# Moving the key and value loads, one split and two score products in the first 35 passes of an attention-then-two-MLPs kernel

## The chip, the cores and the metric

The program runs on one core of one Trainium2 chip, in one launch. The metric is the device time of one execution in microseconds (us), from the runs of the kernel as a whole. Five engines work side by side, each through its own instructions in order: PE (TensorE, matmuls), DVE (VectorE), ACT (ScalarE), POOL (GpSimd) and SP (SyncE, which here issues all DMAs). Semaphores tie them together.

## The reference

For 8 batches, 8 heads, 576 tokens and head width 64, the keys and values are averaged over groups of 8 tokens (576 to 72), and each token attends to the 72 pooled ones. The result, 4608 tokens by 512, goes through two MLPs (512 to 2048 to 512) with a gate each.

```python
k_p = k.reshape(B, H, Sp, pool, D).mean(axis=3)
v_p = v.reshape(B, H, Sp, pool, D).mean(axis=3)
scores = scale * np.matmul(q, k_p.transpose(0, 1, 3, 2))
...
attn = attn / (np.sum(attn, axis=-1, keepdims=True) + 1e-09)
return np.matmul(attn, v_p).astype(np.float32)
...
h = x @ w_in
g = h * (1.0 / (1.0 + np.exp(-h)))     # second MLP: h * clip(h + 3, 0, 6) / 6
return (g @ w_out).astype(np.float32)
```

## The kernel before

The 4608 tokens are 36 tiles of 128 (tile t holds rows 128t to 128t+127, so tile 9 is the first of batch 2 and tile 13 the first with rows of batch 3). Four tiles make a group of 512 tokens, nine groups in all. The kernel has three stretches: attention together with the first layer of the first MLP (to about 493 us), that MLP's second layer (L805), and the second MLP (L721, L821). The change lies in the first stretch.

**Passes.** That stretch is a list of passes n. Pass n computes one block of 128 hidden features for one group: `h_mm`, 12 matmuls of 128x512 at L628 into one of four PSUM banks. Passes 0 to 6 take features 0 to 6 of group 0, passes 7 to 13 the same of group 1, passes 14 to 22 the rest of group 0, 23 to 31 the rest of group 1; then one group after the other. Passes 0 to 6 run in `opening`, the others in the loop below it. Each pass's product goes through a tanh on ACT (L641) and a product on DVE (L642), both written in the next pass, and a store to DRAM on SP (L646). Because there are four banks, pass n needs that DVE product of pass n-4.

**A weight block** is split into two parts once: scale on ACT (L126), three bit operations on DVE (L133, L136, L140), head on ACT (L147), tail on DVE (L152). From pass 24 on, pieces of other weights are prepared in the same way in `pair_slots` (ACT L185, DVE L191 to L198, ACT L214, DVE L218) with sums on POOL (L223).

**An attention tile t** takes these steps, each in a pass that the table `todo` fixes: scores on PE (L458, 8 matmuls into two banks `aps`), maxima on DVE (L502, L505), eight exponentials on ACT (L512), which free the two banks, normalization on DVE (L529 to L533), transposes in blocks of 32 on DVE (L566), which a DMA takes to DRAM (L571, called "out" here) and three DMAs bring back reordered (L577, "back"), the product with the pooled values on PE (L592, `weighted`), and a split of the result into two parts on ACT (L608) and DVE (L609). For group 2 (tiles 8 to 11) the passes of scores and `weighted` are the table

```python
s, w = ((12, 25), (16, 26), (18, 28), (20, 29))[i]
```

with the maxima and exponentials in s+1, the normalization and transposes in s+3, "out" in s+4 and "back" in s+5.

**Keys and values of batch b**, four pieces j each, are loaded in the passes of `kv_in`, k and v together, and pooled on POOL three passes later (`pool_k`: L381, L382, two of L385; `pool_v`: L402, L403, L404). All k pieces share one staging tile and all v pieces another, so a load waits on SP until POOL is through with the piece before; everything that stands behind it on SP waits too. In a pass, the loads stand ahead of the "out" and "back" jobs (`due`) and of the stores (`later`). On POOL, the poolings of a pass stand behind the L223 sums of that pass.

**Before pass 0** the tiles 0 to 3 are worked off; the values of batch 0 are pooled by matmuls with the identity (`summed_v`, L395) for j = 0 and 3, and by POOL for j = 1 and 2. `keep_warm` (L444) issues idle matmuls, `WARM[t+1]` of them ahead of tile t's transposes.

Of the kernel before, what the change touches and what calls it, by code (L numbers as in the profile page):

```python
# [19 lines left out]
POOL = 8  # L20
GT = 512
G2 = 576
WARM = (16, 0, 4, 6)
FILL = 288


# [1 line left out]
def kernel(  # L28
# [815 lines left out]
    for t in range(TPG, NTILE):  # L844
        g, i = divmod(t, TPG)
        if g == 1:
            if i > 1:
                todo.setdefault(i - 1, []).append(("scores", t))
            for n, what in ((i, "soft"), (i + 1, "norm"), (i + 1, "probs"), (max(i + 2, 3), "weighted"), (max(i + 3, 4), "split")):
                todo.setdefault(n, []).append((what, t))  # L850
            continue
        if g == 2:
            s, w = ((12, 25), (16, 26), (18, 28), (20, 29))[i]
        else:
            w = NF * (g - 1) + (4, 7, 10, 13)[i]
            s = w - 10
        start[t] = s
        jobs = [(s, "scores"), (s + 1, "soft"), (w, "weighted"), (w + 1, "split")]
        jobs += [(s + 3, "norm"), (s + 3, "turn")]
        for n, what in jobs:  # L860
            if n >= 0:
                todo.setdefault(n, []).append((what, t))
    kv_in = {}
    for b in range(2, B):
        for j in range(NPAIR):
            n = 6 + 2 * j if b == 2 else start[first_tile[b]] - 18 + 4 * j
            assert n not in kv_in
            kv_in[n] = (b, j)
    stages = {}
    for f in range(1, NF):  # L870
        n = f - 1 if f < FIRST else (6, 7, 8, 10, 11, 13, 15, 17, 19)[f - FIRST]
# [4 lines left out]
    with tc.manual_schedule():  # L876
# [32 lines left out]
        for i in range(2):  # L909
            nc.gpsimd.memset(prs[i][:, H * SP:], 0.0)  # L910
        pool_k(0, 3, nc.gpsimd)
        for j in range(1, NPAIR - 1):
            pool_v(0, j)
        banks = [
            [(ps_a, "a"), (ps_a, "a")], [(ps_h, "h"), (ps_h, "h")],
            [(ps_y, "y0"), (ps_y, "y1")], [(ps_y, "y2"), (ps_y, "y3")],
# [19 lines left out]
        def soft(t):  # L936
            new_pr(t, f"o{4 + t}")
            if t < 1:
                max_exps(t, 0, False)
            else:  # L940
                below_max(t, 0)
                exps(t, 0)
            max_exps(t, 1)

        def turn(t):
            if t < 3:
                norm(t, 1 if t else 2)
            probs_T(t, banks[t], f"o{t}", WARM[t + 1] if t < 3 else 0)

# [8 lines left out]
        nc.scalar.activation(*outer, AF.Copy)  # L958
        scores(3, banks[3])
        soft(2)  # L960
        turn(1)
        soft(3)
        split_scale(0)
# [45 lines left out]
        def opening(n, f, now):  # L1009

            def factor(part, run):
                for what, i in stages.get(n, ()):
                    if what == part:
                        run(i)

            ps = h_mm(0, f, n)
            for what, t in now:
                if what == "weighted":
                    i = t - TPG
                    pv[t] = weighted(t, (A, B2)[i // 2][i % 2:])  # L1020
            if n == 0:
                scores(TPG, A, parts=(1,))
                scores(TPG + 1, B2)
                load_q(TPG + 3)
                vps1.append(bank(C, 1))
                summed_v(vps1[0], 1, 0)
                factor("head", split_head)
                factor("head", split_tail)
            for what, t in now:
                if what == "norm":  # L1030
                    norm(t, 2)
            for what, t in now:
                if what == "soft":
                    all_max(t)
            if late_silu:
                silu(*late_silu.pop())
            late_silu.append((0, f, n, ps))
            if n == 1:
                nc.scalar.activation(vp[1][:, :2 * D], vps1.pop()[:SP, :2 * D], AF.Copy)
            for what, t in now:  # L1040
                if what == "split":
                    split_x(t, pv.pop(t))
            if n:
                factor("head", split_head)
                factor("head", split_tail)
            for what, t in now:
                if what == "soft":
                    new_pr(t)
                    all_exps(t)
            factor("bits", split_bits)  # L1050
            for what, t in now:
                if what == "probs":
                    probs_T(t, C)
            for what, t in now:
                if what == "scores":
                    scores(t, B2 if t % 2 else A)
                    load_q(t + 2)
            factor("scale", split_scale)

        for n, (g, f) in enumerate(order):  # L1060
# [3 lines left out]
            load_ahead(2)  # L1064
            if n >= BEGIN - 3:
                load_halves()
            if n in kv_in:
                load_k(*kv_in[n])
                load_v(*kv_in[n])
            for job in due.pop(n, ()):  # L1070
                job()
            while later:
# [1 line left out]
            now = todo.get(n, ())  # L1074
            if n < FIRST:
                opening(n, f, now)
                if n - 3 in kv_in:
                    pool_k(*kv_in[n - 3], nc.gpsimd)
                    pool_v(*kv_in[n - 3])
                continue  # L1080
            for what, t in now:
                if what == "soft":
# [39 lines left out]
                    split_tail(i)  # L1122
            if job:
                job[1](job[2])
            if n - 3 in kv_in:
                pool_k(*kv_in[n - 3], nc.gpsimd)
                pool_v(*kv_in[n - 3])
            if g == NG - 2 and f in (8, 10):
                next_wide(1)
            if g == NG - 1:  # L1130
# [311 lines left out]
```

## Time and profile before

| what | us |
|---|---|
| median of 3 runs (lowest, highest) | 1508.34 (1507.77, 1509.56) |
| the profiled execution, its own time | 1504.98 |
| its span, first to last instruction | 1503.2 |
| PE busy in the span | 1483.7 (99%) |
| DVE, ACT, POOL busy | 1235.9, 804.2, 325.3 |

The profile is of one execution, whose time is 3.36 us under the median of the runs. The span leaves out what lies around the first and last instruction (1.8 us). Matmuls are pipelined, so that a busy PE need not be one at its peak; its idle time, on the other hand, is time in which it waited. Times in the rows are counted from the start of the span.

### The profile page before, as it was taken

What the parts mean: (1) busy time and instruction counts of PE and PEld (TensorE: products, weight loads), DVE (VectorE), ACT (ScalarE), POOL (GpSimd) and SP (SyncE); (2) the same over time, 40 slices, a digit from 0 to 9 for tenths busy, and PEclk for the clock granted to TensorE, in tenths of its full rate; (3) what the DMA queues carried; (4) which work ended last, traced back from release to release, by engine and by line L of the source; (5) the groups of instructions that cost most, each with busy time, mean ns of one, the idle gap of its engine ahead of it and who ended that gap; (6) DMA issues with size and microseconds to landing.
All of it is one profiled execution on the core that took longest, in us unless ns stands there. A gap on an engine that the chain in (4) does not pass through costs nothing.

```text
span 1503.2 us, 30700 instructions
## 1 busy us (share of the span) xinstructions
PE 1483.7 (99%) x11562; PEld 1415.5 (94%) x11562; DVE 1235.9 (82%) x1883; ACT 804.2 (53%) x1779; POOL 325.3 (22%) x378
## 2 busy tenths in 40 slices
PE   8899999999999999999999999999999999999998
PEld 7678888888888999999999999999999999999998
DVE  7987789788776898888988698888876877777776
ACT  5755555556644544444443677777776444444443
POOL 6362443443011000000000343444440000000000
PEclk9999999999999999999999999999999999999999
DMA  9568889989789955555559866655689954444440
GB/s 308 194 187 266 265 275 295 292 288 315 253 305 373 358 190 183 180 180 179 186 169 355 294 217 207 203 195 199 207 260 320 375 158 142 140 142 142 138 138 29
DMA packets 225461, 342.17 MB, mean 228 GB/s; under 512 B 16800, under 2 KB 157984, under 8 KB 225312
## 3 DMA queue, kind: packets, MB, share of 16 engines
q1 hardware_dynamic: 225312, 340.20, 68.1%
q8 instruction: 91, 1.49, 0.4%
q14 instruction: 58, 0.48, 0.1%
HBM read 194.90 MB, written 145.23 MB: 226 GB/s over the span
## 4 chain that ended last, share of the span: by engine, by line
PE 93%; DMA 3%; DVE 3%; issue 1%; ACT 0%; SPq 0%; DVEq 0%; ACTq 0%
PE pl L805 22%; PE pl L821 22%; PE hps L628 22%; PE py L721 12%; PE pa L721 6%; PE ph L721 3%; PE aps L458 2%; PE aps L592 2%; DVE rw L136 1%; DMA wraw<-in_moe_w_in_dram 1%; DMA qT<-in_q_dram 1%; DMA ro<-in_v_dram 1%; DMA stage<-in_k_dram 1%; DMA stage<-in_v_dram 0%; DVE rs L642 0%
## 5 line engine op out<-in xcount | busy, mean ns | idle before, releaser
L628 PE MATMUL hps<-rx,whl 128*128 128x512 f32 x1728 | 388.5, 383 | 3.1 <-DVE rx L609 2.2
L628 PEld LDWEIGHTS hps<-rx,whl 128*128 128x128 f32 x1728 | 324.2, 190 | 51.4 <-issue 2.6
L805 PEld LDWEIGHTS pl<-rx,wst 128*128 128x128 f32 x3024 | 337.9, 192 | 0.1
L805 PE MATMUL pl<-rx,wst 128*128 128x256 f32 x3024 | 337.9, 275 | 0.0
L821 PE MATMUL pl<-wst,rx 128*128 128x256 f32 x3024 | 337.8, 275 | 0.0
L821 PEld LDWEIGHTS pl<-wst,rx 128*128 128x128 f32 x3024 | 337.8, 192 | 0.0
L223 POOL TENSOR_TENSOR rw<-rw 128x256 f32<-128x256 f32 x96 | 75.7, 796 | 580.1 <-DVE rw L218 550.1
L721 PE MATMUL py<-rx,wst 128*128 128x288 f32 x1152 | 151.8, 286 | 0.2 <-DVE rx L695 0.2
L642 DVE SCALAR_TENSOR_TENSOR rs<-rs,hps 128x512 f32<-128x512 f32 x144 | 98.0, 681 | 61.6 <-ACT rs L641 61.2
L721 PEld LDWEIGHTS py<-rx,wst 128*128 128x128 f32 x1152 | 145.4, 189 | 0.4 <-DVE rx L695 0.4
L791 ACT ACTIVATE rx<-ro 128x1024 fp32r<-128x1024 f32 x86 | 90.6, 1062 | 87.7 <-PE pl L805 35.6
L641 ACT ACTIVATE rs<-hps 128x512 f32<-128x512 f32 x144 | 86.5, 606 | 67.9 <-PE hps L628 67.6
L1158 DVE TENSOR_TENSOR rs<-rs,pl 128x512 f32<-128x512 f32 x90 | 61.6, 685 | 69.6 <-PE pl L821 47.2
L792 DVE TENSOR_TENSOR rx<-ro,rx 128x1024 fp32r<-128x1024 f32 x86 | 103.5, 1224 | 14.6 <-ACT rx L791 14.4
L512 ACT ACTIVATE pr<-aps,mxa 128x72 f32<-128x72 f32 x256 | 78.2, 331 | 45.9 <-DVE mxa L505 45.9
L1161 ACT ACTIVATE rs<-pl 128x512 f32<-128x512 f32 x36 | 21.6, 601 | 145.4 <-PE pl L821 76.1
L791 ACT ACTIVATE rx<-ra 128x1024 fp32r<-128x1024 f32 x70 | 73.7, 1064 | 47.1 <-PE pl L805 18.3
L792 DVE TENSOR_TENSOR rx<-ra,rx 128x1024 fp32r<-128x1024 f32 x70 | 83.3, 1219 | 9.8 <-ACT rx L791 9.8
L791 ACT ACTIVATE rx<-rb 128x1024 fp32r<-128x1024 f32 x63 | 66.3, 1062 | 44.5 <-PE pl L821 20.3
L214 ACT ACTIVATE rw<-rw 128x256 fp32r<-128x256 f32 x152 | 61.8, 417 | 45.0 <-POOL rw L223 24.0
L792 DVE TENSOR_TENSOR rx<-rb,rx 128x1024 fp32r<-128x1024 f32 x63 | 75.9, 1231 | 5.9 <-ACT rx L791 5.8
L218 DVE TENSOR_TENSOR rw<-rw 128x256 fp32r<-128x256 f32 x152 | 71.9, 482 | 8.5 <-ACT rw L214 8.5
(135 smaller groups left out, 2115.6 us busy)
## 6 DMA issues: line engine op xcount, KB each, us to landing
ws<-rw SPq DMA_DIRECT2D x152, 256.0 KB
wst<-ws SPq DMA_DIRECT2D x76, 512.0 KB
g<-rs SPq DMA_DIRECT2D x144, 256.0 KB
g<-rs SPq DMA_DIRECT2D x128, 288.0 KB
ro<-g SPq DMA_DIRECT2D x49, 512.0 KB
ra<-g SPq DMA_DIRECT2D x38, 512.0 KB
rb<-g SPq DMA_DIRECT2D x37, 512.0 KB
rw<-in_moe_w_out_dram SPq DMA_DIRECT2D x64, 256.0 KB
```

What stands on the lines that cost most here:

```text
L214: nc.scalar.activation(t[:, 0], mag, AF.Copy)
L218: nc.vector.tensor_tensor(out=t[:, 1], in0=mag, in1=t[:, 0].bitcast(F32), op=ALU.subtract)
L223: nc.gpsimd.tensor_tensor(out=out, in0=a, in1=b, op=op)
L512: nc.scalar.activation(p_t[t][:, a, i], s_t[t][a][:, i], AF.Exp, scale=ESCALE, bias=mx[:, h], accum_out=den_of(t)[:, h],)
L628: nc.tensor.matmul(ps, w[:, c, :], shuffled(x[:, c, :]), start=(c == 0 and n == 0), stop=(c == NKC - 1 and n == 2),)
L641: nc.scalar.activation(in_two(t), dealt(ps), AF.Tanh)
L642: nc.vector.scalar_tensor_tensor(out=in_two(t), in0=in_two(t), scalar=1.0, in1=dealt(ps), op0=ALU.add, op1=ALU.mult)
L721: nc.tensor.matmul(ps[j], w[:, j, a, c, :], shuffled(x[:, b, c, :]), start=(first and n == 0 and c == 0), stop=(n == 2 and c == 1), skip_g ...
L791: nc.scalar.activation(t[:, dd, 0], src, AF.Copy)
L792: nc.vector.tensor_tensor(out=t[:, dd, 1], in0=src, in1=t[:, dd, 0].bitcast(F32), op=ALU.subtract)
L805: nc.tensor.matmul(ps[:, c * HW:(c + 1) * HW], w[:, b, c * P:(c + 1) * P], shuffled(t[:, dd, a, i]), start=(dd == 0 and c == 0 and i == 0 ...
L821: nc.tensor.matmul(ps[:, c * HW:(c + 1) * HW], t[:, dd, a, i, c * P:(c + 1) * P], shuffled(w[:, b]), start=(dd == 0 and c == 0 and i == 0 ...
```

## The change

Five things change. (1) `kv_in` becomes two tables. For batch 2 the k pieces stay at passes 6, 8, 10, 12 and the v pieces move from these to 15, 17, 19, 21. For batch 3 both were at 11, 15, 19, 23; k is now at 13, 17, 21, 25 and v at 23, 25, 27, 29. Each is pooled three passes after its load. Later batches keep their passes. (2) Tile 7 is split (L608, L609) in pass 5, ahead of the exponentials and the bit operations of that pass, not in pass 6. (3) Scores of tile 10 move from pass 18 to 19 and of tile 11 from 20 to 22, and all that hangs on them moves along: maxima and exponentials, normalization, "out", "back", and the load of q two tiles on. Their `weighted` stays in passes 28 and 29. (4) Piece j = 2 of the values of batch 0 is pooled by eight matmuls and one copy on ACT (now L964), not by POOL. (5) The four idle matmuls ahead of tile 1's transposes go.

```diff
-WARM = (16, 0, 4, 6)
+WARM = (16, 0, 0, 6)
...
-            for n, what in ((i, "soft"), (i + 1, "norm"), (i + 1, "probs"), (max(i + 2, 3), "weighted"), (max(i + 3, 4), "split")):
+            for n, what in ((i, "soft"), (i + 1, "norm"), (i + 1, "probs"), (max(i + 2, 3), "weighted"), (max(i + 3, 4) - (i == 3), "last" if i == 3 else "split")):
...
-            s, w = ((12, 25), (16, 26), (18, 28), (20, 29))[i]
+            s, w = ((12, 25), (16, 26), (19, 28), (22, 29))[i]
...
-    kv_in = {}
+    k_in, v_in = {}, {}
     for b in range(2, B):
         for j in range(NPAIR):
-            n = 6 + 2 * j if b == 2 else start[first_tile[b]] - 18 + 4 * j
-            assert n not in kv_in
-            kv_in[n] = (b, j)
+            n = start[first_tile[b]] - 18 + 4 * j
+            for kv, at in ((k_in, {2: 6 + 2 * j, 3: 13 + 4 * j}), (v_in, {2: 15 + 2 * j, 3: 23 + 2 * j})):
+                at = at.get(b, n)
+                assert at > max(kv, default=0)
+                kv[at] = (b, j)
...
-        for j in range(1, NPAIR - 1):
-            pool_v(0, j)
+        pool_v(0, 1)
...
         soft(2)
+        v2 = bank(A, 1)
+        summed_v(v2, 0, 2)
+        nc.scalar.activation(vp[0][:, 4 * D:6 * D], v2[:SP, 4 * D:6 * D], AF.Copy)
         turn(1)
...
             for what, t in now:
+                if what == "last":
+                    split_x(t, pv.pop(t))
+            for what, t in now:
                 if what == "soft":
                     new_pr(t)
                     all_exps(t)
...
-            if n in kv_in:
-                load_k(*kv_in[n])
-                load_v(*kv_in[n])
+            if n in k_in:
+                load_k(*k_in[n])
+            if n in v_in:
+                load_v(*v_in[n])
...
-            if n - 3 in kv_in:
-                pool_k(*kv_in[n - 3], nc.gpsimd)
-                pool_v(*kv_in[n - 3])
+            if n - 3 in k_in:
+                pool_k(*k_in[n - 3], nc.gpsimd)
+            if n - 3 in v_in:
+                pool_v(*v_in[n - 3])
```

SP, passes 23 to 25 before: the last load of batch 3's keys and values (`stage_1433`, `stage_1435`), then "back" of tile 10 (`bl0`), "out" and "back" of tile 11 (`bl1`).

```order
L368 DMA stage_1433<-in_k_dram 128x576
L376 DMA stage_1435<-in_v_dram 72x1024
L577 DMA ro_187<-bl0_89 32x4x256 x2
L577 DMA ro_187<-bl0_89 8x4x256
L646 DMA g0_0_175<-rs_186 128x2x256
L571 DMA bl1_90<-stage_1459 128x768
L646 DMA g0_0_175<-rs_186 128x2x256
L577 DMA ro_187<-bl1_90 32x4x256 x2
L577 DMA ro_187<-bl1_90 8x4x256
```

SP, passes 25 to 27 of the change: the loads of v pieces 1 (`stage_1461`) and 2 (`stage_1547`) of batch 3, and tile 11's "out" and "back" (`bl1`).

```order
L368 DMA stage_1459<-in_k_dram 128x576
L376 DMA stage_1461<-in_v_dram 72x1024
L646 DMA g0_1_176<-rs_186 128x2x256
L175 DMA rw_188<-in_moe_w_out_dram 128x512
L571 DMA bl1_90<-stage_1495 128x768
L646 DMA g0_1_176<-rs_186 128x2x256
L424 DMA qT_1539<-in_q_dram 128x512
L175 DMA rw_188<-in_moe_w_out_dram 128x512
L376 DMA stage_1547<-in_v_dram 72x1024
L577 DMA ro_187<-bl1_90 32x4x256 x2
L577 DMA ro_187<-bl1_90 8x4x256
```

Tile 11's trip now stands between and behind two loads of v that each wait for POOL; before, no load stood between its "out" and its "back".

POOL, pass 26 before: the first L223 sum, then the last k and v piece of batch 3.

```order
L223 TENSOR_TENSOR rw_188<-rw_188 128x256
L381 TENSOR_TENSOR stage_1433<-stage_1433 128x72x4
L382 TENSOR_TENSOR stage_1433<-stage_1433 128x72x2
L385 TENSOR_TENSOR kbd0_80<-stage_1433 64x72 x2
L402 TENSOR_TENSOR stage_1435<-stage_1435 72x2x256
L403 TENSOR_TENSOR stage_1435<-stage_1435 72x2x128
L404 TENSOR_TENSOR vp0_83<-stage_1435 72x128
```

POOL, passes 26 to 28 of the change: v piece 0 (`stage_1400`), k piece 3 (`stage_1459`) and v piece 1 (`stage_1461`) of batch 3.

```order
L223 TENSOR_TENSOR rw_188<-rw_188 128x256
L402 TENSOR_TENSOR stage_1400<-stage_1400 72x2x256
L403 TENSOR_TENSOR stage_1400<-stage_1400 72x2x128
L404 TENSOR_TENSOR vp0_83<-stage_1400 72x128
L381 TENSOR_TENSOR stage_1459<-stage_1459 128x72x4
L382 TENSOR_TENSOR stage_1459<-stage_1459 128x72x2
L385 TENSOR_TENSOR kbd0_80<-stage_1459 64x72 x2
L402 TENSOR_TENSOR stage_1461<-stage_1461 72x2x256
L403 TENSOR_TENSOR stage_1461<-stage_1461 72x2x128
L404 TENSOR_TENSOR vp0_83<-stage_1461 72x128
```

Three v pieces of batch 3 were pooled ahead of this sum; now all four stand behind it.

DVE, passes 25 and 26 before, from the bit operations of the first weight piece to the tail (L218) that releases the L223 sum.

```order
L191 TENSOR_SCALAR rw_188<-rw_188 128x256
L194 SCALAR_TENSOR_TENSOR rw_188<-rw_188 128x256
L198 SCALAR_TENSOR_TENSOR rw_188<-rw_188 128x256
L642 SCALAR_TENSOR_TENSOR rs_186<-rs_186,hps_1491 128x512
L609 TENSOR_TENSOR rx_185<-aps_1504,rx_185 128x4x128
L191 TENSOR_SCALAR rw_188<-rw_188 128x256
L194 SCALAR_TENSOR_TENSOR rw_188<-rw_188 128x256
L198 SCALAR_TENSOR_TENSOR rw_188<-rw_188 128x256
L218 TENSOR_TENSOR rw_188<-rw_188 128x256
```

The same place of the change (the first two rows are the end of the first bit operations).

```order
L194 SCALAR_TENSOR_TENSOR rw_188<-rw_188 128x256
L198 SCALAR_TENSOR_TENSOR rw_188<-rw_188 128x256
L529 TENSOR_SCALAR den_1410<-den_1410 128x8
L532 RECIPROCAL den_1410<-den_1410 128x8
L533 TENSOR_TENSOR pr1_87<-pr1_87,den_1410 128x576
L566 STREAM_TRANSPOSE stage_1495<-pr1_87 128x256 x3
L642 SCALAR_TENSOR_TENSOR rs_186<-rs_186,hps_1470 128x512
L609 TENSOR_TENSOR rx_185<-aps_1483,rx_185 128x4x128
L191 TENSOR_SCALAR rw_188<-rw_188 128x256
L194 SCALAR_TENSOR_TENSOR rw_188<-rw_188 128x256
L198 SCALAR_TENSOR_TENSOR rw_188<-rw_188 128x256
L218 TENSOR_TENSOR rw_188<-rw_188 128x256
```

Tile 11's normalization and transposes (L529 to L566) now stand ahead of that tail; before they were through two passes earlier.

## Rows read from the trace of the kernel before

**Rows 1.** The page, part 4: the chain that ended last, by engine.

```profile
PE 93%; DMA 3%; DVE 3%; issue 1%; ACT 0%; SPq 0%; DVEq 0%; ACTq 0%
```

**Rows 2.** Waits of PE: engine line waited for, us in total, times, longest.

```profile
PE aps L458 <- ACT pr L512: 3.4, 1, 3.4
PE hps L628 <- DVE rx L609: 2.2, 1, 2.2
```

**Rows 3.** Timeline of PE: start us, length us, what, [idle before <-who ended it].

```profile
48.00 1.25 PE L458 MATMUL aps<-kbd,qT 128*128 128x144 f32 x8 [0.53 <-DMA qT<-in_q_dram]
...
68.00 15.81 PE L628 MATMUL hps<-rx,whl 128*128 128x512 f32 x72 [2.19 <-DVE rx L609]
...
95.87 5.44 PE L628 MATMUL hps<-rx,whl 128*128 128x512 f32 x24
104.74 2.54 PE L458 MATMUL aps<-kbd,qT 128*128 128x144 f32 x8 [3.44 <-ACT pr L512]
106.90 7.42 PE L628 MATMUL hps<-rx,whl 128*128 128x512 f32 x24
...
128.19 1.09 PE L592 MATMUL aps<-ro,vp 72*64 72x128 f32 x16
...
143.19 1.09 PE L592 MATMUL aps<-ro,vp 72*64 72x128 f32 x16
```

**Rows 4.** Windows of 5 us: busy per engine, granted TensorE clock, DMA share, GB/s.

```profile
105.00:110.00 5.00, 5.00 (x15) 4.19 (x16) 3.88 (x9) 2.57 (x10) 1.44 (x2) 0.50 0.68 211
```

**Rows 5.** Timeline of DVE, passes 6 to 26.

```profile
65.13 1.61 DVE L140 SCALAR_TENSOR_TENSOR rw<-wraw,rw 128x512 uint32<-128x512 uint32 x1
...
69.78 0.84 DVE L140 SCALAR_TENSOR_TENSOR rw<-wraw,rw 128x512 uint32<-128x512 uint32 x1
...
99.70 1.68 DVE L136 SCALAR_TENSOR_TENSOR rw<-wraw,rw 128x512 uint32<-128x512 uint32 x1
...
102.13 0.81 DVE L502 TENSOR_REDUCE mxa<-aps 128x4 f32<-128x288 f32 x2
...
121.76 0.17 DVE L529 TENSOR_SCALAR den<-den 128x8 f32<-128x8 f32 x1
...
124.01 0.65 DVE L642 SCALAR_TENSOR_TENSOR rs<-rs,hps 128x512 f32<-128x512 f32 x1
...
130.57 0.28 DVE L191 TENSOR_SCALAR rw<-rw 128x256 uint32<-128x256 uint32 x1
...
131.81 0.42 DVE L218 TENSOR_TENSOR rw<-rw 128x256 fp32r<-128x256 f32 x1
```

**Rows 6.** Timeline of POOL, passes 5 to 26.

```profile
64.48 1.72 POOL L402 TENSOR_TENSOR stage<-stage 72x512 f32<-72x512 f32 x1
...
96.28 1.81 POOL L402 TENSOR_TENSOR stage<-stage 72x512 f32<-72x512 f32 x1 [0.86 <-DMA stage<-in_v_dram]
...
132.30 0.73 POOL L223 TENSOR_TENSOR rw<-rw 128x256 f32<-128x256 f32 x1 [14.09 <-DVE rw L218]
...
135.13 1.28 POOL L402 TENSOR_TENSOR stage<-stage 72x512 f32<-72x512 f32 x1
...
137.30 0.46 POOL L404 TENSOR_TENSOR vp<-stage 72x128 f32<-72x128 f32 x1
```

**Rows 7.** Timeline of ACT: first exponential of tile 9, and the tanhs behind the last.

```profile
103.38 0.31 ACT L512 ACTIVATE pr<-aps,mxa 128x72 f32<-128x72 f32 x1
...
105.75 1.13 ACT L641 ACTIVATE rs<-hps 128x512 f32<-128x512 f32 x2
```

**Rows 8.** Timeline of SP (start us, us in which it issued, line, DMA).

```profile
92.44 0.32 SPq L376 DMA_DIRECT2D stage<-in_v_dram  x1
...
125.10 0.47 SPq L571 DMA_DIRECT2D bl<-stage  x1
...
130.01 1.58 SPq L577 DMA_DIRECT2D ro<-bl  x3
```

**Rows 9.** Waits of SP's DMA queue over the whole span.

```profile
SPq L376 <- POOL vp L404: 19.6, 11, 3.8
```

More of the change, by code (lines that the diff above doesn't have):

```diff
@@ L1124 @@
                 job[1](job[2])
-            if n - 3 in kv_in:
-                pool_k(*kv_in[n - 3], nc.gpsimd)
-                pool_v(*kv_in[n - 3])
+            if n - 3 in k_in:
+                pool_k(*k_in[n - 3], nc.gpsimd)
+            if n - 3 in v_in:
+                pool_v(*v_in[n - 3])
             if g == NG - 2 and f in (8, 10):
```

## Prediction

> **What bounds the kernel now.** I read the page first, then the waits of PE, then PE's timeline, then the timelines of DVE, ACT, POOL and SP around the few places where PE stands still. PE carries 93% of the chain that ended last [rows 1], so a change is worth what PE waits less, or more. In the first stretch two waits stand out after 50 us: 2.2 us for tile 7's split on DVE and 3.4 us for the exponentials of tile 9 on ACT [rows 2]. The reader is to see them as gaps: PE starts pass 7 at 68.00 after 2.19 us idle, and tile 10's scores at 104.74 after 3.44 us [rows 3]. The second costs more than it says. Pass 18 ended at 95.87 + 5.44 = 101.31, pass 19 starts at 106.90, and eight score matmuls take 1.25 at most (48.00): 5.59 - 1.25 = 4.3 us lost, since the second bank came free later than the first. After it the granted clock is 0.50, the lower level of 1.2 GHz [rows 4], and 24 matmuls take 7.42 instead of 5.44: another 2.0. So 2.2 + 4.3 + 2.0 = 8.5 us are what passes 7 to 20 could give back. From 128.19 to the end of the stretch PE runs without a gap.
>
> Ahead of 48.00 the gap was ended by a load of q [rows 3]. So I cost edits 4 and 5 (v0 by matmuls, no idle matmuls) at nothing: 8 short matmuls for 4 idle ones and three POOL operations fewer are hidden by the loads that end at 48.00. If those landed sooner, the 0.53 us of that gap is the most that could show, either way.
>
> **Tile 7's split (edit 2).** L609 of tile 7 moves ahead of the three bit operations (L140 alone 0.84 [rows 5]) and of one L642 (0.65) on DVE, so it ends an estimated 3 us sooner. Pass 6 then ends after the split, and pass 7 starts without the 2.19 us. The sum of DVE's work is unchanged: only the bit operations come later, by one split. Passes 7 to 18 come 2.2 earlier on PE, with DVE's products still ahead of them by one to five us.
>
> **The moved poolings (edit 1), seen from DVE.** Between 62 and 102 us DVE works nearly all the time, and six of its operations take much longer than their like: the first is L140 at 65.13, 1.61 for 0.84, while POOL runs L402 of a v piece (64.48, 1.72), the last L136 at 99.70, 1.68 [rows 5, 6]. Together these six waits are 4.0 us; three stand in v poolings, three in k poolings. In the changed order four k pieces of batch 2, one of batch 3 and one v piece are left in this stretch. I count four hits of 0.65, 2.6 us: a gain of 1.4. So tile 9's maxima, at 102.13 before, start at 100.7. The bounds are 0 (as many hits as before) and 4.0.
>
> The page "SBUF — State Buffer" of the Trainium skill, section "Who interferes with whom", says that the port which POOL shares with DVE is an exclusive lock: whoever comes first keeps it for its whole instruction, and the other blocks. The trace agrees in kind (0.77 us more inside a 1.72 us pooling). It speaks against the change: a pooling that is moved takes its lock along, and each moved one can cost as much where it lands. What that would give is the second rival.
>
> **Scores of tiles 10 and 11 later (edit 3), seen from PE.** Exponentials follow the maxima by 1.25 and take 2.4 for a tile (102.13, 103.38, 105.75) [rows 5, 7]. With maxima at 100.7, tile 9's banks come free at 103.3 and 104.3. PE asks for them at 101.31 - 2.2 + 2.7 (one pass more) = 101.8. It waits 1.5, then for the second bank, in all some 2.1 us, in pieces shorter than the 2.19 that left the clock up. Tile 11's scores, at 112.6, wait in the same way for tile 10's exponentials (112.1 to 114.6), some 1.6. Of the 8.5 us 4.8 are then gained: `weighted` of tile 8, at 128.19 before, would start near 123.4, and that of tile 11, 15.0 later [rows 3], would be asked for at 138.4.
>
> **What is late next.** That last step is where I expect the gain to go. Tile 11's "back" has to land before its `weighted`. Before, its "out" was issued at 125.10 and "back" at 130.01, done by 131.6, for a use at 143.19 [rows 3, 8]. Now it stands on SP behind the load of v piece 2, which waits for POOL to be through with piece 1, whose load waits for piece 0, whose pooling stands behind the first L223 sum on POOL, which waits for the tail L218 of pass 26 on DVE. That SP stands still in such waits is in the trace: 19.6 us, 11 times, in front of v loads [rows 9].
>
> When is that L218? Following DVE from 100.7: maxima and exponentials of tile 9 to 104.3; tanh and L642 to 105.5; three bit operations (2.1, with some wait 2.4), L642 0.6, normalization and transposes 2.25 (121.76 to 124.01), a tail and tile 10's maxima 1.5, to 112.1. Exponentials to 114.6, tanh, two L642 by 116.5, normalization of tile 10 and maxima of tile 11 3.15, to 119.65. Exponentials to 122.05, tanh and two L642 with ACT's pace 2.15, the half piece's bits 1.25 (130.57 to 131.81), to 125.45. Now tile 11's normalization and transposes, 2.25, to 127.7; L642 and tile 8's split 1.2, bits 1.25, tail 0.45: 130.6, against 132.30 before [rows 5, 6].
>
> From there: L223 0.7; pooling of piece 0 2.63 (135.13 to 137.76); load of piece 1 from issue to the start of its pooling 3.84 (92.44 to 96.28); its pooling 2.63; issue of piece 2 and "back" 0.3 + 1.6; semaphores 0.1: 11.8 us [rows 6, 8]. The landing of "back" is in no row. At least it is 0; at most it is what the 384 KB "out" took, 4.9 (125.10 to 130.01), and I take 2.5, as its pieces are a third of that size. So "back" lands at 130.6 + 11.8 + 2.5 = 144.9. The page "DMA: Bandwidth & Descriptors", section "Anatomy of one DMA — SWDGE (gpsimd) path", of the Trainium skill gives 2.0 us and bytes over 436 GB/s for a DMA of another queue; by an estimate from it 128 KB would land after 2.3 and the sum be 0.2 lower; no run here shows it.
>
> **The sum.** `weighted` of tile 11 starts at 144.9 instead of 143.19: +1.7. PE has then waited 6.5 us, longer than the 3.44 that brought the clock down, and I add the 2.0 that it cost there (between 0, if it stays up, and 3). After that PE does what it did before, and two products per bank of slack hide the rest. 1.7 + 2.0 = +3.7 us: 1508.7 for the profiled execution of 1504.98, or **1512.0** against the median of 1508.34 (the profile stands 3.4 below it). Its own range: DVE 2 us sooner or later, the poolings slowed by DVE by up to 1 each, the landing between 1 and 4, the clock 0 to 3: 1509 to 1515.5. About 0.2%, 3 us, is what a measurement of this kernel can tell from no change.
>
> **Rivals.**
> First, faster: the wait at tile 11's `weighted` is short. It decides at L218: if DVE loses nothing more to POOL and is not held by ACT between tiles 10 and 11, L218 follows `weighted` of tile 8 as closely as before (128.19 to 132.30), and PE with all of the 8.5 us gained gives L223 at 123.8, 126 with tile 11's normalization ahead. Then "back" lands at 126 + 14.3 = 140.3, 2.9 earlier than 143.19, after a wait of some 5.6 from 134.7; with a landing in 1 us and the clock kept up 138.8, or 4.4 earlier. For it: POOL stood idle for 14.09 us ahead of that L223 [rows 6], so nothing on POOL itself holds it up. Against: six waits of DVE on POOL don't vanish, and the order puts more on DVE there. 1503.9 to 1507.5, say 1504.5.
>
> Second, slower by more, by the lock: the poolings cost DVE as much as before where they land, no gain of 1.4, and 0.4 more in each of two v poolings (1.72 against 1.28, L402) [rows 6]. L223 at 132.0, "back" at 147.1, with the clock 1508.34 + 3.9 + 2.0 = 1514.2.
>
> Third, no difference: the same chain, but the clock stays up or L218 is 2 us sooner: +1.7 or so, 1508 to 1510. That edits 4 and 5 do not show in the time at all is part of every case.
>
> **Chances.** The forecast 0.38, slower by the lock 0.12, no difference 0.28, faster 0.22. Of the forecast's 0.38 some 0.06 lies within 3 us, of the third rival 0.03 beyond it on the slow side. Faster 0.22, within 0.2% 0.31, slower 0.47. The range takes the faster rival down to 1503.0 and the lock up to 1515.5; beyond lie some 0.1 on each side.
>
> **What would show it.** Right: PE's waits for L609 and the 3.4 us for tile 9's exponentials gone or halved; a new wait of PE at L592 for DMA `ro<-bl`, 4 to 8 us, near 138 us; SP's waits of v loads on POOL L404 longer, two of some 10 us ahead of "back"; a window of clock 0.5 after it, none at 105. Wrong: no PE wait at L592, or "back" issued before 138; or DVE's L136, L140 and L152 with fewer than two long ones between 62 and 102, so that L223 starts before 127.

## The result and the profile after

The change makes the kernel slower: a median of 1514.98 us (1513.52 to 1519.66, 6 runs) against 1508.05 (1505.38 to 1509.56, 6 runs); ratio 1.0056, 95% interval 1.0041 to 1.0071, that is 6 to 11 us. The ratio is not the quotient of the medians: these lie 6.9 us apart, and 0.56% is 8.4 us. The forecast was 1512.0, +3.7: the sign was right, the size about half of what was measured; 1514.98 lies in the stated range, near its slow end. The profiled execution has a span of 1511.7 us instead of 1503.2.

In short: PE comes earlier to tile 8's product, as intended, and then stands still for 9.5 us in front of tile 11's, because the DMAs that bring tile 11's probabilities back stand on SP behind loads of v that wait for POOL.

Waits of PE in the changed kernel behind the first 45 us, in the columns of [rows 2]:

```profile
PE aps L592 <- DMA ro<-bl: 9.5, 1, 9.5
PE aps L458 <- ACT pr L512: 2.1, 4, 0.6
PE hps L628 <- DVE whl L152: 1.4, 1, 1.4
PE aps L458 <- DMA qT<-in_q_dram: 1.3, 1, 1.3
```

Both waits that the change aimed at are gone: tile 7's split is in no row, and the 3.4 us for tile 9's exponentials have become four pieces of 0.6 at most, two for tile 9's and two for tile 10's. A single new wait, 9.5 us for tile 11's "back", outweighs them. Timeline of PE, as in [rows 3]; the last row is the start of the second stretch:

```profile
48.82 1.25 PE L458 MATMUL aps<-kbd,qT 128*128 128x144 f32 x8 [1.30 <-DMA qT<-in_q_dram]
...
102.90 0.76 PE L458 MATMUL aps<-kbd,qT 128*128 128x144 f32 x4 [0.64 <-ACT pr L512]
104.09 0.76 PE L458 MATMUL aps<-kbd,qT 128*128 128x144 f32 x4 [0.44 <-ACT pr L512]
...
112.28 2.00 PE L628 MATMUL hps<-rx,whl 128*128 128x512 f32 x8 [1.38 <-DVE whl L152]
...
124.52 1.09 PE L592 MATMUL aps<-ro,vp 72*64 72x128 f32 x16
...
149.05 1.97 PE L592 MATMUL aps<-ro,vp 72*64 72x128 f32 x16 [9.46 <-DMA ro<-bl]
150.78 2.12 PE L458 MATMUL aps<-kbd,qT 128*64 128x144 f32 x16
152.83 8.04 PE L628 MATMUL hps<-rx,whl 128*128 128x512 f32 x36
...
500.31 19.93 PE L805 MATMUL pl<-rx,wst 128*128 128x256 f32 x177
```

The last two of these in the kernel before:

```profile
145.20 8.04 PE L628 MATMUL hps<-rx,whl 128*128 128x512 f32 x36
...
492.48 27.79 PE L805 MATMUL pl<-rx,wst 128*128 128x256 f32 x247
```

Where the 8.5 us of the span come from, by these rows against those of before (in brackets the time in the changed kernel, then before): the scores behind the q load start 0.82 later (48.82, 48.00). From there to tile 8's `weighted` the changed kernel gains 4.49 (75.70, 80.19). From that to tile 11's `weighted` it loses 9.53 (24.53, 15.00). From there to the second stretch it loses 1.97 (351.26, 349.29); 0.7 is left for the rest. The 1.97 is mostly the clock: the two products behind the wait take 1.97 and 2.12, and the next pass starts 3.78 behind tile 11's `weighted` instead of 2.01. The windows show the granted clock at 0.50, the lower level of 1.2 GHz, after PE has stood still (columns of [rows 4]):

```profile
140.00:145.00 5.00, 0.00 (x0) 0.00 (x0) 3.21 (x7) 2.19 (x5) 3.83 (x5) 0.75 0.90 298
145.00:150.00 5.00, 0.95 (x10) 0.98 (x12) 2.83 (x8) 0.00 (x0) 2.21 (x3) 0.50 1.05 262
150.00:155.00 5.00, 5.00 (x36) 4.41 (x33) 2.46 (x6) 2.46 (x12) 0.38 (x1) 0.73 0.80 238
```

Why "back" is late is on three engines. DVE, from the bit operations behind tile 9's maxima to the tail that releases the first sum:

```profile
105.16 1.37 DVE L133 TENSOR_SCALAR rw<-rw 128x512 uint32<-128x512 uint32 x1
106.57 1.22 DVE L136 SCALAR_TENSOR_TENSOR rw<-wraw,rw 128x512 uint32<-128x512 uint32 x1
...
125.06 0.69 DVE L642 SCALAR_TENSOR_TENSOR rs<-rs,hps 128x512 f32<-128x512 f32 x1 [0.24 <-ACT rs L641]
125.66 0.82 DVE L191 TENSOR_SCALAR rw<-rw 128x256 uint32<-128x256 uint32 x1
126.52 0.94 DVE L194 SCALAR_TENSOR_TENSOR rw<-rw 128x256 uint32<-128x256 uint32 x1
...
129.19 1.10 DVE L566 STREAM_TRANSPOSE stage<-pr 128x256 f32<-128x256 f32 x3
...
131.38 0.27 DVE L191 TENSOR_SCALAR rw<-rw 128x256 uint32<-128x256 uint32 x1
...
132.62 0.44 DVE L218 TENSOR_TENSOR rw<-rw 128x256 fp32r<-128x256 f32 x1
```

POOL, from two poolings of batch 2 that the change moved to passes 20 and 24, to that sum and the ends of the next two v pieces:

```profile
104.98 1.27 POOL L402 TENSOR_TENSOR stage<-stage 72x512 f32<-72x512 f32 x1 [0.75 <-DMA stage<-in_v_dram]
...
125.06 1.27 POOL L402 TENSOR_TENSOR stage<-stage 72x512 f32<-72x512 f32 x1
126.41 0.73 POOL L403 TENSOR_TENSOR stage<-stage 72x256 f32<-72x256 f32 x1
...
133.14 0.73 POOL L223 TENSOR_TENSOR rw<-rw 128x256 f32<-128x256 f32 x1 [5.41 <-DVE rw L218]
...
135.97 0.45 POOL L404 TENSOR_TENSOR vp<-stage 72x128 f32<-72x128 f32 x1
...
142.49 0.45 POOL L404 TENSOR_TENSOR vp<-stage 72x128 f32<-72x128 f32 x1
```

SP, its loads of v pieces 0, 1 and 2 of batch 3 (L376), tile 11's "out" (L571) and "back" (L577):

```profile
127.76 0.34 SPq L376 DMA_DIRECT2D stage<-in_v_dram  x1
...
136.46 0.33 SPq L376 DMA_DIRECT2D stage<-in_v_dram  x1
...
137.81 0.39 SPq L571 DMA_DIRECT2D bl<-stage  x1
...
142.97 0.33 SPq L376 DMA_DIRECT2D stage<-in_v_dram  x1
143.35 1.19 SPq L577 DMA_DIRECT2D ro<-bl  x3
```

Read them together: the loads of pieces 1 and 2 are issued a few hundredths behind the end of a pooling (136.42 and 136.46, 142.94 and 142.97), and "out" and "back" right behind the loads. Tile 11's transposes are through at 130.29, but its "out" goes at 137.81. SP's waits of v loads on POOL rose from 19.6 us [rows 9] to 28.1.

### The profile page after: what moved, and what is told of

The parts are those of the page before. It is cut to its first block, busy times and chain, and to the rows that moved or that the text cites. A ratio compares the mean times of both kernels' runs of the same rounds, so it can differ in the third digit from the quotient of the medians.

```text
span 1511.7 us, 30726 instructions
## 1 busy us (share of the span) xinstructions
PE 1484.3 (98%) x11574; PEld 1416.4 (94%) x11574; DVE 1234.4 (82%) x1883; ACT 802.0 (53%) x1780; POOL 318.0 (21%) x375
## 4 chain that ended last, share of the span: by engine, by line
PE 87%; DVE 5%; DMA 4%; issue 1%; ACT 1%; POOL 1%; SPq 0%; DVEq 0%; ACTq 0%; POOLq 0%
PE pl L821 22%; PE pl L805 22%; PE hps L628 19%; PE py L721 11%; PE pa L721 6%; PE ph L721 3%; PE aps L592 2%; PE aps L458 2%; DMA wraw<-in_moe_w_in_dram 1%; DMA qT<-in_q_dram 1%; ACT pr L512 1%; DMA ro<-in_v_dram 1%; DMA stage<-in_k_dram 1%; DVE rw L136 1%; DVE rs L642 1%
## 5 line engine op out<-in xcount | busy, mean ns | idle before, releaser
L628 PE MATMUL hps<-rx,whl 128*128 128x512 f32 x1728 | 386.5, 382 | 2.6 <-DVE whl L152 1.4
L628 PEld LDWEIGHTS hps<-rx,whl 128*128 128x128 f32 x1728 | 322.8, 189 | 50.4 <-issue 2.1
L223 POOL TENSOR_TENSOR rw<-rw 128x256 f32<-128x256 f32 x96 | 75.1, 789 | 567.7 <-DVE rw L218 537.6
L642 DVE SCALAR_TENSOR_TENSOR rs<-rs,hps 128x512 f32<-128x512 f32 x144 | 97.8, 681 | 67.9 <-ACT rs L641 67.3
L792 DVE TENSOR_TENSOR rx<-rb,rx 128x1024 fp32r<-128x1024 f32 x63 | 75.9, 1230 | 5.9 <-ACT rx L791 5.8
L218 DVE TENSOR_TENSOR rw<-rw 128x256 fp32r<-128x256 f32 x152 | 72.8, 488 | 9.3 <-ACT rw L214 9.3
```

The costliest lines, as they stand in the source:

```text
L218: nc.vector.tensor_tensor(out=t[:, 1], in0=mag, in1=t[:, 0].bitcast(F32), op=ALU.subtract)
L223: nc.gpsimd.tensor_tensor(out=out, in0=a, in1=b, op=op)
L628: nc.tensor.matmul(ps, w[:, c, :], shuffled(x[:, c, :]), start=(c == 0 and n == 0), stop=(c == NKC - 1 and n == 2),)
L642: nc.vector.scalar_tensor_tensor(out=in_two(t), in0=in_two(t), scalar=1.0, in1=dealt(ps), op0=ALU.add, op1=ALU.mult)
L792: nc.vector.tensor_tensor(out=t[:, dd, 1], in0=src, in1=t[:, dd, 0].bitcast(F32), op=ALU.subtract)
```

## The experiments

Each experiment is a kernel with a part of the change or another order. Theory A, which most of them test: what is lost is tile 11's wait, and it comes from v loads that wait on SP for POOL ahead of "out" and "back". Each kernel was timed against the kernel before. The table is from the timelines of PE: the start of the scores behind the q load (q), of tile 8's `weighted` (w8), the wait in front of tile 11's (w11) and its start, and the start of the second stretch. Each row is of one profiled execution, the ratio of all runs.

| kernel | q | w8 | w8 - q | wait at w11 | w11 | second stretch | ratio (95%) |
|---|---|---|---|---|---|---|---|
| before | 48.00 | 128.19 | 80.19 | 0 | 143.19 | 492.48 | 1 |
| changed | 48.82 | 124.52 | 75.70 | 9.46 | 149.05 | 500.31 | 1.0056 (1.0041, 1.0071) |
| v3_later | 50.16 | 127.42 | 77.26 | 1.29 | 143.79 | 500.56 | 1.0070 (1.0056, 1.0083) |
| back_first | 51.02 | 128.96 | 77.94 | 7.41 | 151.45 | 502.72 | 1.0044 (1.0031, 1.0058) |
| old_tables | 51.34 | 131.68 | 80.34 | 0 | 146.69 | 496.80 | 1.0002 (0.9991, 1.0012) |
| v_earlier | 50.13 | 128.36 | 78.23 | 4.17 | 147.73 | 500.15 | 1.0040 (1.0025, 1.0056) |
| v0_alone | 50.44 | 133.32 | 82.88 | 0 | 148.32 | 498.14 | 1.0013 (1.0001, 1.0024) |
| split_alone | 47.37 | 128.44 | 81.07 | 0 | 143.44 | 492.76 | 1.0010 (1.0000, 1.0020) |
| scores_alone | 48.18 | 126.72 | 78.54 | 0 | 141.73 | 491.85 | 1.0004 (0.9993, 1.0016) |
| spaced | 50.99 | 128.82 | 77.83 | 0 | 144.03 | 496.34 | 1.0015 (1.0003, 1.0027) |
| again (before) | 48.71 | 128.22 | 79.51 | 0 | 143.22 | 492.50 | 0.9997 (0.9986, 1.0008) |
| warm_kept | 50.14 | 130.84 | 80.70 | 0 | 145.85 | 495.13 | 1.0006 (0.9994, 1.0018) |
| no_v0 | 48.59 | 124.63 | 76.04 | 8.81 | 148.51 | 500.30 | 1.0046 (1.0031, 1.0060) |
| best | 51.84 | 130.40 | 78.56 | 0.45 | 146.00 | 495.42 | 0.9986 (0.9977, 0.9996) |

Two things blur the column w8 - q. The kernel before, run again, has 79.51 for 80.19. And in back_first, v0_alone, spaced and best the clock fell at q: the first 12 matmuls of L628 behind it took 4.70, 4.96, 3.85 and 4.15 us for the 2.85 of the others, and `weighted` behind them started 1.9 to 3.0 us later. Without that spaced would have 75.9 and best 76.3, v0_alone 79.9 and back_first 75.2.

**v3_later.** Only the passes of v:

```diff
-(v_in, {2: 15 + 2 * j, 3: 23 + 2 * j})
+(v_in, {2: 15 + 2 * j, 3: (23, 28, 31, 34)[j], 4: 36 + 3 * j})
```

> The changed kernel, but v pieces 1 to 3 of batch 3 are loaded in passes 28, 31 and 34 instead of 25, 27 and 29 (batch 4's v in 36, 39, 42, 45), so that none stands between tile 11's out and back on SP. Theory A (SP's chain of v loads costs it): tile 11's weighted waits for nothing or under 1 us, the start of tile 8's weighted stays near 124.5 as in the change, and its lead of 3.7 us over the kernel before is kept: about 1504.5 us, ratio 0.9975. Rival B (DVE is slowed by POOL wherever the v pieces are pooled, and that sets the end): PE waits somewhere else between 124 and 153 us, ratio 1.002 or more. Rival C (the DMAs themselves are slow then, whatever stands ahead): back still lands 4 to 6 us after its issue, but that alone costs nothing if it is issued by 134.

Tile 11's wait fell from 9.46 to 1.29, a little over what I expected, and yet the kernel is as slow as the change or slower: 1.0070 for an expected 0.9975. Its timeline of PE:

```profile
143.79 1.09 PE L592 MATMUL aps<-ro,vp 72*64 72x128 f32 x16 [1.29 <-DMA ro<-bl]
...
185.81 1.09 PE L592 MATMUL aps<-ro,vp 72*64 72x128 f32 x16 [1.61 <-DMA ro<-bl]
...
222.40 1.12 PE L592 MATMUL aps<-ro,vp 72*64 72x128 f32 x16 [3.66 <-DMA ro<-bl]
```

The wait is of the same kind, at later tiles: with loads three passes apart, each one asks for the staging tile while the piece before it is still to be pooled, and "out" and "back" stand behind it there. So theory A holds at tile 11, and my expectation of the time missed that I had moved the same queue, not emptied it.

**back_first.** In pass 27 alone, the due jobs (here tile 11's "back") ahead of the loads:

```diff
+            if n == 27:
+                for job in due.pop(n, ()):
+                    job()
             if n in k_in:
                 load_k(*k_in[n])
```

> The changed kernel with one swap: in pass 27 tile 11's back stands ahead of the load of v piece 2 on SP; the wait of piece 1's load in pass 25 stays ahead of its out. Theory A has two links, and this takes the second away: back is issued when out has landed, about 4.5 us after 137.8, so near 142.4 instead of 143.35, and without the 288 KB of the v piece ahead of it may land up to 1.2 sooner: PE's wait falls from 9.5 to between 7 and 8.5 us, time 1 to 2.2 us under that of the change, ratio 1.004 to 1.005. If the load of piece 2 were the whole cause, PE's wait would be under 5.

The wait is 7.41, the ratio 1.0044: as expected of two links. The profile puts this wait down to tile 12's transposes on DVE, which end at 151.42, just ahead of `weighted` at 151.45. But `weighted` of tile 11 reads nothing that they write, and it does read what "back" brings, so I take it for a wait on "back". SP in this kernel:

```profile
140.51 0.33 SPq L376 DMA_DIRECT2D stage<-in_v_dram  x1
...
141.86 0.38 SPq L571 DMA_DIRECT2D bl<-stage  x1
...
146.08 1.18 SPq L577 DMA_DIRECT2D ro<-bl  x3
147.35 0.32 SPq L376 DMA_DIRECT2D stage<-in_v_dram  x1
```

"Out" still stands behind the load of piece 1, and "back" follows it after 4.2 us, ahead of piece 2. Part of the smaller wait is PE's own lateness: it asked 93.0 us after q here and 90.8 in the change, since the clock had fallen at q in this execution.

**old_tables.** Edits 2 to 5 with the old loads (the one-line edit puts `6 + 2 * j` and `11 + 4 * j` in for both k and v).

> The changed kernel with the old passes for all loads and poolings of batches 2 and 3 (6, 8, 10, 12 and 11, 15, 19, 23, k and v together): the other four edits alone. Theory A: no wait at tile 11's weighted. POOL's poolings are back between 62 and 102 us and cost DVE the 2.4 us more that the trace of before shows there (4.0 against 1.6), so the scores of tile 10 wait 2 to 4 us, and the lead at tile 8's weighted is 1 to 2 instead of 3.7: ratio 0.998 to 0.9995. Rival B (the poolings' place doesn't matter to DVE): lead 3.7 and ratio 0.9975. Rival D (the loss comes from the scores' new passes, not from the loads): a wait of over 3 us at tile 11's weighted, ratio over 1.001.

No wait at tile 11, and no lead at tile 8 either (80.34): the ratio is 1.0002, a little above the range that I gave. Without the moved poolings the gain of edits 2 and 3 is taken back ahead of tile 8: PE waits 3.16 us for exponentials at tile 10 and 1.34 for a k pooling at tile 9. So most of the 4.5 us needs the moved poolings, and the same move cost the 9.5. Rivals B (lead 3.7 with the old poolings) and D (a wait at tile 11 from the later scores) are out. Edit 1 alone was not run.

**v_earlier.**

```diff
-(v_in, {2: 15 + 2 * j, 3: 23 + 2 * j})
+(v_in, {2: 9 + 2 * j, 3: 17 + 2 * j})
```

> The changed kernel with v of batch 2 in passes 9, 11, 13, 15 and of batch 3 in 17, 19, 21, 23, still apart from k: all v pieces but the last are pooled ahead of the first sum on POOL in pass 26, so no load waits for that sum ahead of tile 11's back. Theory A: no wait at tile 11's weighted (under 1 us). Between 62 and 102 us four more v poolings stand on POOL than in the change, each of which costs DVE some 0.4 to 0.8 as in the trace of before: lead at tile 8's weighted 1.5 to 3.5, ratio 0.9975 to 0.999. Rival B: PE waits elsewhere between 100 and 150 us for DVE or ACT, by 3 us or more, ratio 1.0 to 1.003.

A miss: 4.17 us at tile 11 and 1.0040 for an expected 0.9975 to 0.999, though no load ahead of tile 11's trip waits for the first L223 any more. The last load of v stands right ahead of tile 10's "out" and waits for a piece that POOL reaches in the next pass (its L404 ends at 131.89):

```profile
131.92 0.34 SPq L376 DMA_DIRECT2D stage<-in_v_dram  x1
132.31 0.34 SPq L571 DMA_DIRECT2D bl<-stage  x1
...
136.21 1.16 SPq L577 DMA_DIRECT2D ro<-bl  x3
...
139.45 0.44 SPq L571 DMA_DIRECT2D bl<-stage  x1
...
144.12 1.18 SPq L577 DMA_DIRECT2D ro<-bl  x3
```

Tile 10's "back" waits here for its "out", and everything of tile 11 comes behind it on the same queue. The L223 sum was one thing that holds a load; a pooling that is simply not due yet is another.

**v0_alone, split_alone, scores_alone.** The kernel before with edits 4 and 5, with edit 2, and with edit 3.

> The kernel before with edits 4 and 5 alone (v piece 2 of batch 0 by matmuls, no idle matmuls). In the five profiles with these edits the first scores behind the q load start at 48.8 to 51.3 us (48.82, 50.16, 51.02, 51.34, 50.13) against 48.00 in the one without. Theory E (these edits make the opening later): that start lies at 50 or above again, and the time is 1 to 3 us longer, ratio 1.0007 to 1.002. Rival F (the loads of the opening end at another time in every execution, whatever the kernel): the start lies anywhere from 47.5 to 51, in the two kernels beside it as well, and the ratio is within 0.999 to 1.001.

> The kernel before with edit 2 alone (tile 7's split in pass 5). The wait of 2.2 us at pass 7 goes. My prediction counted it as gained. Theory G (between 50 and 125 us DVE is what PE runs against): PE comes 2.2 sooner to tile 10's scores and waits 2.2 longer there, 5.6 instead of 3.4, so that tile 8's weighted is 80.2 us behind the start at 48 as before: no change, ratio 0.999 to 1.0005. Rival (the gain is kept): 78.0 and ratio 0.9985. The start at 48 tells theory E from F too: 48.0 within 0.5 by E.

> The kernel before with edit 3 alone (scores of tile 10 in pass 19, of tile 11 in pass 22, and what hangs on them). Theory G: one pass more, 2.7 us, is taken off the wait of 3.4, and the clock stays up: tile 8's weighted 76 to 78 us behind the start near 48 instead of 80.2. With the old loads no load of v stands between tile 11's out and its back, so its weighted waits under 1 us: 2 to 4 us gained, ratio 0.9975 to 0.9987. Rival H (later scores make tile 11's trip too late by themselves): a wait of 2 us or more at its weighted, ratio 1.0 or above.

split_alone has the time that theory G expects, though not quite by its way. The wait at pass 7 is gone, and PE waits instead at tile 9 for a k pooling on POOL and at tile 10 for exponentials, where the kernel before waited 3.44:

```profile
95.79 0.51 PE L458 MATMUL aps<-kbd,qT 128*128 128x144 f32 x2 [2.18 <-POOL kbd L385]
...
105.95 0.76 PE L458 MATMUL aps<-kbd,qT 128*128 128x144 f32 x4 [2.79 <-ACT pr L512]
```

Of 2.2 us nothing is left at tile 8 (81.07 for 80.19), and the ratio is 1.0010 (expected up to 1.0005). scores_alone has the lead at tile 8 (78.54, somewhat less than expected) and no wait at tile 11, which rules out rival H, but its ratio of 1.0004 can't be told from no change, which misses the expected gain. v0_alone starts q at 50.44 and is 0.13% slower, as theory E expects, with an interval that barely leaves out no change.

**spaced.** Loads that are to meet a free staging tile, and the tiles' trips ahead of them:

```diff
-(v_in, {2: 15 + 2 * j, 3: 23 + 2 * j})
+(v_in, {2: 15 + 2 * j, 3: (25, 29, 33, 35)[j], **{c: 23 + 16 * (c - 3) + 4 * j for c in range(4, 8)}})
...
+            for job in due.pop(n, ()):
+                job()
             if n in k_in:
                 load_k(*k_in[n])
             if n in v_in:
                 load_v(*v_in[n])
-            for job in due.pop(n, ()):
-                job()
```

> The changed kernel, with v loads that meet a free staging tile and stand behind the tiles' trips: v of batch 3 in passes 25, 29, 33, 35, of batches 4 to 7 every fourth pass from 39, 55, 71 and 87, and in every pass out and back ahead of the loads on SP. Theory A: tile 11's weighted waits under 1 us, and so do those of tiles 12 to 18, which waited 1.6 and 3.7 us when v pieces of batches 3 and 4 followed each other in three passes. Tile 8's weighted then stands 75 to 76.5 us behind the start of the first scores after the q load, as in the change, and nothing takes it back: 4 us better than before from there on, less what the opening loses (0.8 to 3.3): ratio 0.997 to 0.9995. If a wait of over 3 us for back is still there, SP's loads are not its cause.

No `weighted` of the stretch waits for "back", and the ratio falls from the change's 1.0056 to 1.0015 by these edits alone: theory A in its cleanest form. The loads still wait for POOL, 23.8 us in all (28.1 in the change), so the staging tile is not always free; but none of these waits holds a trip long enough to reach PE. How much spacing and order each do was not run apart. The time missed its range (0.997 to 0.9995), and the rows show two losses: q was late and the clock fell there, and tile 13 waits for the last v piece, which I had loaded too late:

```profile
50.99 2.29 PE L458 MATMUL aps<-kbd,qT 128*128 128x144 f32 x8 [4.16 <-DMA qT<-in_q_dram]
...
179.32 0.34 PE L592 MATMUL aps<-ro,vp 72*64 72x64 f32 x4 [2.97 <-POOL vp L404]
```

**again, warm_kept, no_v0.** The kernel before once more; edit 4 without edit 5; edits 1 to 3.

> The kernel before, once more, for the spread of its opening and of its time. Theory E (edits 4 and 5 make the opening later): its first scores behind the q load start at 47.4 to 48.2 us, as in the three profiles without those edits (48.00, 47.37, 48.18). Rival F (it varies by itself): outside of that, up to 51. Ratio 0.999 to 1.001.

> The kernel before with edit 4 alone: v piece 2 of batch 0 by matmuls, the four idle matmuls kept. Theory I (the missing idle matmuls make the opening later): the start behind the q load is at 48.2 or under, ratio 0.9995 to 1.0005. Rival J (the matmuls in place of POOL's sum do it): at 49.5 or above, ratio 1.0005 to 1.002.

> The changed kernel without edits 4 and 5: edits 1 to 3. By theories A and E together the loss has two parts that add up: the opening (about 2 us) and the wait at tile 11's weighted. Without the first the scores behind the q load start at 48.2 or under, the wait at tile 11's weighted is still 9 to 10 us, and the ratio is 1.0035 to 1.0045 instead of 1.0056. If the opening doesn't add to the rest (the wait swallows it), the ratio stays at 1.005 or above.

again has q at 48.71, outside of what theory E allows, and its time is as expected. warm_kept has q at 50.14 and a ratio of 1.0006, which is rival J's side; its interval takes in no change. no_v0 keeps nearly the whole loss: 8.81 us at tile 11, ratio 1.0046, each just outside of what I expected. With old_tables, split_alone and scores_alone near no change, this puts most of the result on edit 1, with edits 2 and 3 in place, and on the wait that it makes. Edits 4 and 5 are worth 0.10% between the changed kernel and this one, 0.13% alone, 0.06% with the idle matmuls kept; each interval reaches to, or nearly to, nothing.

**best.** As spaced, without edits 4 and 5, v of batch 3 in passes 25, 28, 31, 34.

> Edits 2 and 3, batch 2's loads as in the change, no edits 4 and 5, and v of batch 3 in passes 25, 28, 31, 34, of batches 4 to 7 every fourth pass from 39, 55, 71 and 87, with out and back ahead of the loads in every pass. By theories A and E nothing is left that takes the lead back: the scores behind the q load start at 48.2 or under, tile 8's weighted 75.5 to 77 us behind that (80.2 before), no wait over 1 us at any weighted (tile 13 waited 3.0 for v piece 3 with its load in pass 35; now it is pooled a pass sooner), the second stretch starts at 488.5 to 490 instead of 492.48: ratio 0.9965 to 0.9985. If the place of DVE's and POOL's work takes the lead back elsewhere, it is 0.9995 or more.

Faster than both kernels: median 1505.30 against 1507.40, ratio 0.9986 (0.9977 to 0.9996), just past the slow end of the range that I gave. Against no_v0 (1.0046) it differs only in the later v loads and in the order on SP: this pair is the plainest evidence for theory A. From tile 11's `weighted` to the second stretch it takes 349.42 us, as before (349.29). Its profiled execution had a late opening, so that q, w8 - q and the second stretch all missed what I expected; it took 1507.9 us, 2.6 over the median, and does not itself show the gain:

```profile
51.84 2.29 PE L458 MATMUL aps<-kbd,qT 128*128 128x144 f32 x8 [3.19 <-DMA qT<-in_q_dram]
...
146.00 1.09 PE L592 MATMUL aps<-ro,vp 72*64 72x128 f32 x16 [0.45 <-DMA ro<-bl]
```

The first row also falsifies theory E in its strict form: q at 51.84 without edits 4 and 5. Of six profiles without them q starts at 47.37 to 48.71 in five and at 51.84 in one; of eight with both (seven) or with edit 4 alone (warm_kept) at 48.82 to 51.34. The later start goes with what the DMAs moved in the first 14 us; the kernel before, then v0_alone:

```profile
DMA packets 1554, 3.60 MB, mean 257 GB/s; under 512 B 173, under 2 KB 173, under 8 KB 1554
```

```profile
DMA packets 1503, 3.40 MB, mean 243 GB/s; under 512 B 168, under 2 KB 168, under 8 KB 1503
```

In the kernel best it was 3.31 MB. The matmuls of edit 4 start at 17.4 us at the earliest, so they can't be what slows these loads. Whether edits 4 and 5 make a slow opening more frequent, or eight profiles drew it by chance, stays open; it is worth 1 to 2 us of the 8.

## Why the prediction was right in sign and wrong in size

The mechanism was right: the forecast had the place of the new wait (tile 11's `weighted`), its chain (L218, L223, two poolings, two loads, "back"), and the fall of the clock. Two terms of the sum were too small: the time at which L218 ends, and the landing of "back". Point by point:

- **Tile 7's split**: the wait is gone, right. Alone it gave nothing (split_alone); that passes 7 to 18 stay 2.2 earlier is seen only together with the moved poolings.
- **Scores of tiles 10 and 11**: 1.08 (0.64 and 0.44) and 1.02 us of waiting where I had 2.1 and 1.6, the clock up. Tile 9's maxima started at 100.06, not 100.7: between 62 and 102 us three operations of DVE were lengthened by 1.3 us in all, not four by 2.6. A wait that I had not listed, 1.38 for L152 in pass 22, used up most of what these terms had gained. Tile 8's `weighted`: 123.4 forecast, 124.52 measured, of which 0.82 is the opening.
- **The end of L218**: forecast 130.6, measured 133.06. This step failed by 2.5 us. I had DVE's work between tiles 9 and 11 nearly undisturbed, and it met two v poolings of batch 2 that the change had moved there, in passes 20 and 24. At 105.16 the three bit operations took 3.6 us for my 2.4: L133 1.37 and L136 1.22, while POOL pooled a v piece (L402 at 104.98 and what follows it), for 0.42 at 79.05 and 0.84 at 91.81. That lateness stays, so that the L642 ahead of the half piece's bits ended 1.5 later than I had it (125.75 for 124.2). It is behind the late L152 of pass 22 too: DVE has no gap from 104.56 to the end of that L152 at 112.23. Then the half piece's bits took 2.4 us for the 1.25 that I had taken from [rows 5], while POOL ran L402 and L403 of the last batch 2 piece (125.06 to 127.14). That is the lock that I had made a rival of its own and left out of the main sum at these places; that it is the poolings is read from the overlap in time, no run takes them away alone. The Trainium skill's page "SBUF — State Buffer", section "Who interferes with whom", states the rule; the trace agrees, L191 took 0.82 beside this pooling and 0.27 at 131.38 without one.
- **From L223 to the issue of "back"**: 11.5 us (133.06 to 144.54) for my 11.8. Right.
- **The landing**: 2.5 forecast, 4.5 measured (144.54 to 149.05), near the upper bound of 4.9. This is the second term that failed. In six kernels it lay between 2.3 (best) and 5.0 (no_v0); the two longest are those in which 288 KB of v were issued just ahead of it. But in back_first, with that load behind it, it still took 4.2, so the cause is not shown. I had scaled one duration by size, and the runs show that the same three DMAs take twice as long in one kernel as in another.
- **The clock**: 2.0 forecast, 1.77 measured.
- **The sum**: tile 11's `weighted` +1.7 forecast, +5.86 measured (4.2 more: 2.5 from L218, 2.0 from the landing, less 0.3 from L223 to the issue). With the clock and 0.9 of smaller terms that is 8.5 for the profiles; the ratio of the runs gives 8.4, their medians 6.9.
- **Edits 4 and 5 at nothing**: q started 0.82 later where I had allowed 0.53. That bound was too tight for any kernel: the kernel before itself had q 0.71 later in again. What these edits are worth is open.
- **Two sums of mine** are off by 0.15 without weight here: tile 9's first bank comes free at 103.15 by my own steps, not 103.3, and tile 10's maxima are through at 112.25, not 112.1.

The second rival's 1514.2 is next to the measured median, in part by luck: it had the lock take away the gain ahead of tile 9, which came in full (2.7 us for my 1.4), but it was right that the moved poolings cost DVE about as much where they land. It had the landing at 2.5 too.

## What to carry to other kernels

A load into a staging tile whose last content is not yet consumed is a wait for the consumer, and everything behind it on the same queue waits too: here tile 11's "out", which went 7.5 us after its transposes were through (130.29, 137.81). When loads are moved closer together, list what stands behind each on the issuing queue, put short round trips ahead of them, and give each load time until the piece before is consumed; spacing alone only moved the wait (v3_later). Work that is moved away from one place to free an engine can cost that engine again where it lands: of some 2.7 us that DVE gained ahead of tile 9, some 2.5 came back beside the moved poolings. And a wait of the busiest engine is only worth its length if the engine that it waits for is not in step with it: PE's 2.2 us at pass 7 were lost again as soon as POOL and ACT were asked for the next result (split_alone).

## What the runs showed of the hardware that I had not expected

The pace of the first loads differs between executions with the same opening, 3.31 MB (best) to 3.66 MB (no_v0) in 14 us, and the start of the scores behind q goes with it: every profile under 3.45 MB has q at 50.1 or later, every one over 3.52 MB at 48.6 or earlier; of the three between, two have 48.7 and 48.8 and one 50.13.

Idle time of nearly the same length leaves the clock up or not. PE waited 2.60 us in the kernel before and 2.57 in no_v0 ahead of the same eight matmuls, which took 1.04 and 1.89; the granted clock between 40 and 45 us was 1.00 in the one and 0.66 in the other, between the levels of 2.4 and 1.2 GHz since both levels occur in that window:

```profile
40.91 1.04 PE L544 MATMUL aps<-ident,pr 128*72 128x128 f32 x8 [2.60 <-DVE pr L533]
```

```profile
40.84 1.89 PE L544 MATMUL aps<-ident,pr 128*72 128x128 f32 x8 [2.57 <-DVE pr L533]
```

The same shows at pass 7: PE waited 2.19 us there in the kernel before, and the 72 matmuls behind took 15.81 [rows 3]; in again, the same kernel, it waited 2.23 and they took 17.43. So a wait just under the one that brought the clock down is no safe price: I had counted on pieces shorter than 2.19. Nor is the price of a fall fixed: 1.6 us here, 1.77 at tile 11, 1.9 to 3.0 at q.
